# Down and output projections turned: weights held in the array, 512 tokens moving

## The chip, the cores and the metric

The kernel runs on one core of one Trainium2 chip. The metric is the device time of one launch in microseconds, as the median of several runs. Besides the runs there is a profile of one execution, with its trace, in which every instruction of every engine has a start and a length. The engines are TensorE (PE in the profile, with its weight loads as PEld), VectorE (DVE), ScalarE (ACT), GpSimd (POOL) and SyncE (SP). SP, ACT and POOL also issue DMA transfers, each in the order of its own queue. On chip, data lies in SBUF with 128 partitions; products of TensorE go to PSUM, whose eight banks of 128 x 512 fp32 the kernel hands round.

## The reference, cut to what matters

The input x has 2048 tokens of 640 features. A gate g per token mixes two branches: a is attention with a running memory over four segments of 512 tokens (32 heads of 20 features), b is a SwiGLU network with 1728 hidden features.

```python
def _A_ref(x, wq, wk, wv, wo, beta):        # H = 32, Dh = 20, N = 4, L = 512
    g = _sigmoid(beta).reshape(1, H, 1, 1)
    ...
    for s in range(N):
        logits = jnp.einsum("bhqd,bhkd->bhqk", qs, ks) * scale + mask
        p = _softmax(logits, axis=-1)
        a_dot = jnp.einsum("bhqk,bhkd->bhqd", p, vs)
        num = jnp.einsum("bhld,bhde->bhle", pq, M)
        den = jnp.einsum("bhld,bhd->bhl", pq, z)[..., None] + 1e-6
        a_mem = num / den
        o = g * a_mem + (1.0 - g) * a_dot
        M = M + jnp.einsum("bhld,bhle->bhde", pk, vs)
        ...
    return o @ wo

def _B_ref(x, w1, w3, w2):
    h = _silu(x @ w1) * (x @ w3)
    return h @ w2

g = _sigmoid((x * gate_w).sum(-1, keepdims=True))
return g * a + (1 - g) * b
```

## The kernel before

Everything is fp32. A number is split into a high part that TensorE takes in its fp32r format and the remaining low part, and a product is three passes, high x high, high x low and low x high (`PASSES`). The parts of weights are made by ACT (a cast, L115) and POOL (a subtraction, L116). Weights come as rows of 640 columns: `w_add` plans one, a DMA on SP brings it into `wr`, `w_step` advances the loads and splits by a count of work done, and six split rows `W` exist at a time. POOL brings ten of the query and key rows itself (L172).

**What TensorE does.** Its order is written out: generators yield after a piece of work, and a loop weaves them. `head` holds the first projections of tokens 0 to 1023 (chunks 0 and 1, called A). Then four segments `segs` follow; each is a list of jobs (projections, SwiGLU up and down, output projections) between whose pieces slots of `attention()` are put, by a credit of estimated time. `tail` is what is left after the last attention. `braid` puts one step of a generator after every few of another, `chain` joins them. Chunks 2 and 3 (B) come in the second half.

**The other engines.** Their instructions are in the order that a scheduler with a timeline model gives them; those in `here(...)` keep the order of the program. Each engine and each queue is strictly in its order: an instruction that waits holds all behind it.

**SwiGLU down, `ffn_down` (L509 to L535).** Called for five groups of hidden blocks, `GROUPS`, four of three blocks of 128 and one of the last full block and the 64-row rest, and for two chunks each. A tile `f` is 128 tokens x 320 features, a bank in PSUM: the hidden values `ht` of 128 tokens are the weights of the array, and 320 columns of `W` move (L523). Each product with three passes counts three matmuls, the rest two. Four blocks of tokens and two halves make eight tiles per chunk. The first group's eviction is a copy scaled by `cgate` = 1 - g on ACT (L529), the others multiply by `cgate` and add on DVE (L531), into `acc` (128 tokens x 4 blocks x 640). The rooms for accumulators (`slot`, two) are shared with the values `V` of a chunk: V of chunk 2 takes the room of chunk 0's accumulator, chunk 3's accumulator that of chunk 1's, each once its stores have landed. At the very last group (chunks 2 and 3) each block of tokens is stored from SP (L535).

**Attention (`attention`, L717).** Scores `s` and `t`, exps on ACT (`P`, L611), masks by POOL selects (L615), the products `o` with the values (L625). The results, not yet divided by their row sums, go through `oq` to the DRAM buffer `od`, 32 rows a head of which row 20 holds the sums. The memory's transposes `mr` go to `qk` by small DMAs on ACT (L593). POOL loads `qk` (L549).

**Output projection (`oproj`, L744 to L783; `normalize`, L681).** `o_sums` reads the row sums `rs` of a chunk, `o_scale` takes their reciprocals times (1 - sigmoid(beta)) and splits them into three bf16 parts `rp`, and three DMAs on SP put these into `rR` (L668). `normalize` multiplies a constant 0/1 matrix `sel` with `rR` on TensorE (L687, a tile `rr` per block of 128 features): this spreads a head's factor over its 20 features. DVE multiplies `oall` by it (L688), and adds the memory's part (L693), which POOL has read back as `gm` (`load_memory`, L678) and TensorE has turned (`gt`, L692). For chunk 0 there is no memory. `part` splits 128 tokens at a time into `oT`; a tile `op` is 128 tokens x 320 features of 15 matmuls (L768), and DVE multiplies it by the gate and adds it to `acc` (L777).

**Gate.** The projection of values has one more column, gate_w. `v_blocks` takes exp(-x) of it, and makes `gate` = g and `cgate` = 1 - g, one number per token and so per partition.

**Store.** `store(c)` (L785) sends chunks 0 and 1 from POOL's queue, four DMAs of 128 tokens x 640 (L788). `store(0)` is braided into the last down of A and is followed by the projections of q and v of chunk 2; `store(1)` is braided into the first down of B.

## Time and profile before

| what | value |
|---|---|
| median of 3 runs | 1114.06 us (1112.69 to 1115.69) |
| the profiled execution | 1116.25 us |
| its span, first to last instruction | 1114.5 us |
| mean granted clock of TensorE | 0.998 of full speed |
| PE busy | 1098.6 us, 99% of the span |
| PEld, DVE, ACT, POOL busy | 909.3, 591.4, 463.4, 482.3 us |
| DMA | 151.96 MB in 84911 packets, mean 136 GB/s |

A group of instructions in the profile is a line, an engine, an operation, the tile written and the tiles read, with partitions x elements; then the count, the busy time in us and the mean of one in ns; behind the second bar the idle time of the engine just before them and what ended it. Matmuls overlap in these records, so their spacing is read from the chain or a timeline: start, length, what, and how many. A wait names the instruction that waited, what released it, the total in us, the times and the longest. A row of the view of windows has, for each engine, busy us and count (PE, PEld, DVE, ACT, POOL), then the granted clock, the share of DMA and GB/s.

### The profile page before, as it was taken

To read this page: it belongs to the slowest core of one execution; us is meant where nothing else is said; L and a number is where in the kernel's file an instruction comes from. 1 tells how busy PE (TensorE), PEld (TensorE's weight loads), DVE (VectorE), ACT (ScalarE), POOL (GpSimd) and SP (SyncE) were. 2 spreads that over 40 slices of the span, in tenths; PEclk is the share of its full clock that TensorE was granted. 3 is DMA by queue.
4 is the path that set the end of the run, shared out by engine and by line. 5 is a ranking of instruction groups with operands and counts; after the bars stand their busy time and mean duration, and the time that the engine had idled before them with its cause. 6 is when DMAs were issued, how large, how long until landed. Compare 5 with 4: busy or idle time off the path is not lost. (4 is left out here: it accounts for less than half of the span.)

```text
span 1114.5 us, 19295 instructions
## 1 busy us (share of the span) xinstructions
PE 1098.6 (99%) x6953; PEld 909.3 (82%) x6953; DVE 591.4 (53%) x1750; ACT 463.4 (42%) x956; POOL 482.3 (43%) x603
## 2 busy tenths in 40 slices
PE   9999999999999999999999999998999999999998
PEld 6988878877878888988977786788778778877988
DVE  5032564355655544565253677774557666651644
ACT  6255334553343233255255644435534344344040
POOL 5053445355364254354253436434653545444140
PEclk9999999999999999999999999999999999999999
DMA  9275943334265134435285867435753433432122
GB/s 330 83 237 206 267 115 93 83 96 128 59 149 118 51 84 125 121 94 189 94 265 207 297 187 177 115 115 161 170 128 104 115 93 100 115 104 76 49 60 95
DMA packets 84911, 151.96 MB, mean 136 GB/s; under 512 B 11344, under 2 KB 24144, under 8 KB 84816
## 3 DMA queue, kind: packets, MB, share of 16 engines
q1 hardware_dynamic: 60528, 103.40, 29.6%
q0 software_dynamic: 20832, 41.30, 16.1%
q10 hardware_dynamic: 3456, 6.03, 1.5%
q8 instruction: 55, 0.90, 0.3%
q14 instruction: 40, 0.33, 0.1%
HBM read 95.25 MB, written 54.53 MB: 134 GB/s over the span
## 5 line engine op out<-in xcount | busy, mean ns | idle before, releaser
L116 POOL TENSOR_TENSOR W<-wr,W 128x640 fp32r<-128x640 f32 (+1 forms) x126 | 197.4, 1571 | 289.3 <-ACT W L115 229.2
L579 DVE CUSTOM_DVE_ANT_0 junk<-s,mask 128x256 bf16<-128x256 f32 (+3 forms) x512 | 250.5, 489 | 113.0 <-PE s L572 81.4
L611 ACT ACTIVATE P<-t 128x512 f32<-128x512 f32 (+1 forms) x384 | 172.0, 539 | 128.4 <-PE t L605 125.7
L261 PE MATMUL g<-X,W 128*128 128x512 f32 x840 | 207.9, 397 | 0.7 <-ACT P L611 0.7
L523 PE MATMUL f<-W,ht 128*128 128x320 f32 x1312 | 201.9, 313 | 0.3 <-POOL W L116 0.3
L523 PEld LDWEIGHTS f<-W,ht 128*128 128x128 f32 x1312 | 195.9, 190 | 3.1 <-POOL W L116 0.6
L261 PE MATMUL u<-X,W 128*128 128x512 f32 x780 | 197.3, 399 | 0.0
L261 PEld LDWEIGHTS g<-X,W 128*128 128x128 f32 x840 | 155.8, 188 | 36.6 <-ACT P L611 0.9
L615 POOL TENSOR_SCALAR_AFFINE_SELECT P<-P 128x256 f32<-128x256 f32 x192 | 92.5, 492 | 199.0 <-ACT P L611 198.8
L261 PEld LDWEIGHTS u<-X,W 128*128 128x128 f32 x780 | 143.7, 188 | 34.6 <-ACT P L611 0.3
L115 ACT CAST W<-wr 128x640 fp32r<-128x640 f32 (+1 forms) x133 | 95.0, 727 | 111.7 <-PE u L261 27.5
L116 POOL TENSOR_TENSOR ht<-ft,ht 128x512 fp32r<-128x512 f32 x52 | 67.0, 1288 | 86.8 <-ACT ht L115 82.9
L531 DVE SCALAR_TENSOR_TENSOR acc<-f,cgate,acc 128x320 f32<-128x320 f32 x128 | 69.4, 548 | 42.1 <-PE f L523 41.6
L549 POOL DMA_DIRECT2D qk<-qkd x128 | 82.7, 648 | 1.9 <-PE t L605 1.7
L572 PE MATMUL s<-qk 60*128 60x256 f32 (+3 forms) x512 | 76.6, 345 | 1.0 <-DVE fu L492 1.0
L261 PE MATMUL k<-X,W 128*128 128x512 f32 x300 | 76.6, 402 | 0.7 <-ACT P L611 0.7
L625 PE MATMUL o<-P,vg 128*32 128x512 f32 (+3 forms) x1024 | 75.5, 436 | 0.1
L261 PE MATMUL q<-X,W 128*128 128x512 f32 x300 | 73.8, 399 | 0.6 <-DVE X L116 0.4
L768 PE MATMUL op<-W,oT 128*128 128x320 f32 x480 | 74.0, 312 | 0.0
L372 PE MATMUL v<-W,X 128*128 128x320 f32 (+1 forms) x480 | 71.6, 311 | 1.1 <-ACT P L611 1.1
L372 PEld LDWEIGHTS v<-W,X 128*128 128x128 f32 x480 | 71.0, 189 | 1.5 <-ACT P L611 1.3
L768 PEld LDWEIGHTS op<-W,oT 128*128 128x128 f32 x480 | 71.1, 189 | 0.8
(105 smaller groups left out, 1025.3 us busy)
## 6 DMA issues: line engine op xcount, KB each, us to landing
qk<-qkd POOLq DMA_DIRECT2D x128, 240.0 KB, 4.5
wr<-in_w_dram SPq DMA_DIRECT2D x80, 320.0 KB
qkd<-qs SPq DMA_DIRECT2D x20, 512.0 KB
qkd<-ks SPq DMA_DIRECT2D x20, 512.0 KB
od<-oq SPq DMA_DIRECT2D x32, 256.0 KB
wr<-in_wo_dram SPq DMA_DIRECT2D x20, 320.0 KB
vg<-vd SPq DMA_DIRECT2D x16, 336.0 KB
xr<-in_xT_dram SPq DMA_DIRECT2D x20, 256.0 KB
```

Source lines behind the costliest of these rows:

```text
L115: pin(nc.scalar.copy(dst[:, 0], src))
L116: (lo or nc.gpsimd.tensor_sub)(dst[:, 1], src, dst[:, 0].bitcast(F32))
L261: nc.tensor.matmul(ps, w[:, a, kb * P:(kb + 1) * P], x[:, b, kb, :], start=n == 0, stop=n == 14)
L372: nc.tensor.matmul(ps[:, :n1 - n0], x[:, a, kb, lb * P:(lb + 1) * P], wvt[kb][:, b, n0:n1], start=n == 0, stop=n == 14)
L523: nc.tensor.matmul(ps[:, :320], a, b, start=n == 0, stop=n == len(ms) - 1)
L549: here(nc.gpsimd.dma_start(t[64 * i:64 * i + RH], qkd[c][RH * (h + i):RH * (h + i + 1)]))
L572: nc.tensor.matmul(ps[i][:, o:o + w], q[:, qb * P:(qb + 1) * P], key[:, :w], start=n == 0, stop=n == len(todo) - 1, skip_group_check=True)
L579: nc.vector.tensor_tensor_reduce(out=junk[:, :w], in0=ps[i][:, o:o + w], in1=mask[:, L - w:], scale=1.0, scalar=-3.0e38, op0=ALU.add, op1= ...
L611: last["exp"] = nc.scalar.activation(pairs[2 * m + k]["P"][:, i, o:o + n], ps[i][:, b:b + n], AF.Exp, scale=SCALE)
L615: nc.gpsimd.affine_select(d, d, pattern=[[0, 2], [0, n], [1, P]], base=0, channel_multiplier=-1, compare_op=ALU.is_ge, fill=0.0)
L625: nc.tensor.matmul(ps[32 * i:32 * i + 32, kb * P:], heads[2 * p + i]["v"][:, kb], pairs[p + i // 2]["P"][:, i % 2, o:o + n], start=kb == 0 ...
L768: nc.tensor.matmul(ps[:, :320], oT[0][:, qb % 2, a, kb * P:(kb + 1) * P], ws[kb][:, b, 320 * hf:320 * hf + 320], start=n == 0, stop=n == 14)
```

## The change

The two products that end in `acc` change sides. In the down projection 128 output features of `W` are now the weights of the array and the 512 tokens of a chunk move, so a tile is 128 features x 512 tokens, five a chunk (`fb`) for eight; the output projection does the same with `op`. `acc` is 128 x 5 x 512, and the output leaves the chip as chunk, block, feature, token; it is turned back on the host.

A token is now an element of a row and no partition, so the gate can no longer be a factor per partition. Instead of g and 1 - g the kernel keeps e = exp(x) (at most 1e10) and the share s = 1/(1 + e) = 1 - g. Then g a + (1 - g) b = s (e a + b). The ratio e is folded into what becomes a: into the memory's part when it is read (`memory_read`, a second factor of the same instruction) and into the factors of the row sums (`o_scale`). At the end `acc` is multiplied by s. Both go through a small DRAM buffer `ed` (a transfer of 4-byte pieces on ACT's queue) and are read back spread over the partitions: `er`, e for 32 heads, and `sh`, s for 128 partitions (`load_share`).

The factors of the row sums are no longer spread by a product: `o_scale` writes each head's factors 20 times to the DRAM buffer `rd` by four DMAs, and `normalize` reads blocks of 128 rows of it (`rb`), in the same two buffers that `sh` uses. `gm` is loaded by block of features; `oT`'s high parts take its room, the low parts that of `oall`.

For chunks 0 and 1 `store` loads the share, and POOL multiplies each of the five blocks and issues its DMA. For chunks 2 and 3 the last group of `ffn_down` adds, multiplies (alternately on POOL and DVE) and stores from SP; the last tile is done in two halves on DVE.

```diff
...
                 nc.vector.reciprocal(r, r)
-                nc.vector.tensor_mul(
-                    gm.rearrange("p (h e) -> p h e", e=DH),
-                    nd[:, :, :DH], r.unsqueeze(2).broadcast_to([P, 16, DH]))
+                nc.vector.scalar_tensor_tensor(
+                    gm.rearrange("p (h e) -> p h e", e=DH), nd[:, :, :DH], gate[:, c, 1, qb:qb + 1],
+                    r.unsqueeze(2).broadcast_to([P, 16, DH]), op0=ALU.mult, op1=ALU.mult)
                 store_later(gd[c][:, qb, 320 * hf:320 * hf + 320], gm, ("g", c, qb), n=2)
...
                 if hf == 1:
-                    nc.scalar.activation(gate[:, c, lb:lb + 1], ps[:, 320:321], AF.Exp, scale=-1.0)
+                    nc.scalar.activation(gate[:, c, 1, lb:lb + 1], ps[:, 320:321], AF.Exp)
                 yield 450
             store_later(vd[c][:, lb], vv.rearrange("p h e -> p (h e)"), ("v", c, lb), nc.scalar)
-        nc.vector.tensor_scalar(gate[:, c], gate[:, c], 1.0, None, op0=ALU.add)
-        nc.vector.reciprocal(gate[:, c], gate[:, c])
-        nc.vector.tensor_scalar(cgate[:, c], gate[:, c], -1.0, 1.0, op0=ALU.mult, op1=ALU.add)
+        e, g = gate[:, c, 1], gate[:, c, 0]
+        nc.vector.tensor_scalar(e, e, TOP, None, op0=ALU.min)
+        nc.vector.tensor_scalar(g, e, 1.0, None, op0=ALU.add)
+        nc.vector.reciprocal(g, g)
+        store_later(ed[c].rearrange("x a p -> p (x a)"), gate[:, c].rearrange("p x a -> p (x a)"), ("e", c), nc.scalar)
     def k_block(c, mb, i, prev):
...
             if first:
-                accs[c] = slot(f"acc{c}")[:, :4 * D].rearrange("p (b d) -> p b d", b=4)
-            for lb in range(4):
-                for hf in range(2):
-                    ps = bank_tile(f"f{c}_{js[0]}_{lb}_{hf}", 700)
-                    ms = []
-                    for j, w in zip(js, w2s):
-                        for a, b in (PASSES if j < NF else ((0, 0), (0, 1))):
-                            ms.append((hts[c, j][:, a, lb * P:(lb + 1) * P], w[:, b, 320 * hf:320 * hf + 320]))
-                    for n, (a, b) in enumerate(ms):
-                        nc.tensor.matmul(ps[:, :320], a, b, start=n == 0, stop=n == len(ms) - 1)
-                        if n == len(ms) // 2:
-                            yield 149.0 * (n + 1)
-                    filled()
-                    dst = accs[c][:, lb, 320 * hf:320 * hf + 320]
-                    if first:
-                        nc.scalar.activation(dst, ps[:, :320], AF.Copy, scale=cgate[:, c, lb:lb + 1])
-                    else:
-                        nc.vector.scalar_tensor_tensor(dst, ps[:, :320], cgate[:, c, lb:lb + 1], dst,
-                                                       op0=ALU.mult, op1=ALU.add)
-                    yield 149 * (len(ms) - len(ms) // 2 - 1)
-                if last:
-                    nc.sync.dma_start(out[0, c * L + lb * P:c * L + lb * P + P, :], accs[c][:, lb])
+                accs[c] = slot(f"acc{c}")[:, :KB * L].rearrange("p (b n) -> p b n", b=KB)
+            if last:
+                load_share(c)
+            for fb in range(KB):
+                ps = bank_tile(f"f{c}_{js[0]}_{fb}", 1300 if len(js) > 2 else 690)
+                ms = []
+                for j, w in zip(js, w2s):
+                    for a, b in (PASSES if j < NF else ((0, 0), (0, 1))):
+                        ms.append((w[:, b, fb * P:(fb + 1) * P], hts[c, j][:, a, :]))
+                for n, (w, h) in enumerate(ms):
+                    nc.tensor.matmul(ps, w, h, start=n == 0, stop=n == len(ms) - 1)
+                    if n % 3 == 2 and n < len(ms) - 1:
+                        yield 699.0 if n == 2 else 699
+                filled()
+                dst = accs[c][:, fb]
+                if first:
+                    nc.scalar.copy(dst, ps)
+                elif not last:
+                    nc.vector.tensor_add(dst, ps, dst)
+                else:
+                    end = (c, fb) == (cs[-1], KB - 1)
+                    for n0 in ((0, 256) if end else (0,)):
+                        d, p, g = (t[:, n0:n0 + (256 if end else L)] for t in (dst, ps, shares[c]))
+                        nc.vector.tensor_add(d, p, d)
+                        (nc.vector if end or fb % 2 else nc.gpsimd).tensor_mul(d, d, g)
+                        nc.sync.dma_start(out[c, fb, :, n0:n0 + d.shape[-1]], d)
+                yield 699 if len(ms) % 3 == 0 else 466
     oall, heads, pairs = {}, {}, {}
...
     def o_sums(c):
+        assert ("e", c) in stored
         here(nc.sync.dma_start(rs, od[c][:, DH].rearrange("h (a n) -> h a n", n=P)))
+        here(nc.sync.dma_start(er, ed[c][1:2].broadcast_to([H, 4, P])))
         after(16 if c < NSEG - 1 else 3, o_scale, c)
...
         if b == 0:
-            oall[c] = cp.tile([P, KB, L], F32, tag="oall", name=f"oall{c}", bufs=1)
+            oall[c] = cp.tile([P, KB, L], FR, tag="oall", name=f"oall{c}", bufs=1)
         for h, e, n, r in rows(b):
-            dst = oall[c][r:r + n, b]
+            dst = oall[c][r:r + n, b].bitcast(F32)
             if n > DH:
...
         here(nc.vector.reciprocal(rs, rs))
-        nc.vector.tensor_scalar(rs, rs, cR, None, op0=ALU.mult)
-        nc.vector.tensor_copy(rp[:, 0], rs)
-        nc.vector.tensor_sub(rs, rs, rp[:, 0])
-        nc.vector.tensor_copy(rp[:, 1], rs)
-        nc.vector.tensor_sub(rp[:, 2], rs, rp[:, 1])
-        for i in range(3):
-            here(nc.sync.dma_start(rR[32 * i:32 * i + 32].rearrange("h (a n) -> h a n", n=P), rp[:, i]))
+        nc.vector.scalar_tensor_tensor(rs, rs, cR, er, op0=ALU.mult, op1=ALU.mult)
+        for a in range(4):
+            here(nc.sync.dma_start(rd[c][:, :, a * P:(a + 1) * P], rs[a::4].unsqueeze(1).broadcast_to([H, DH, P])))
         turned.append(c)
+    shares = {}
+    def spread(name):
+        return sp.tile([P, L], F32, tag="spread", name=name, bufs=2)
+    def load_share(c):
+        shares[c] = spread(f"sh{c}")
+        here(nc.sync.dma_start(shares[c], ed[c][0].rearrange("a n -> (a n)").unsqueeze(0).broadcast_to([P, L])))
     gms = {}
...
         assert ("g", c, 3) in stored
-        gms[c] = big_tile(f"gm{c}")[:, :4 * D].rearrange("p (b d) -> p b d", b=4)
+        gms[c] = big_tile(f"gm{c}", FR)[:, :KB * L].rearrange("p (b n) -> p b n", b=KB)
         for qb in range(4):
-            here(nc.gpsimd.dma_start(gms[c][:, qb], gd[c][:, qb]))
+            here(nc.gpsimd.dma_start(gms[c].bitcast(F32)[:, :, qb * P:(qb + 1) * P],
+                                     gd[c][:, qb].rearrange("p (b n) -> p b n", b=KB)))
             yield 1
     def normalize(c):
+        rows = rd[c].rearrange("h e n -> (h e) n")
+        rb = {}
+        def load(b):
+            if b < KB:
+                assert c in turned
+                rb[b] = spread(f"rb{c}_{b}")
+                here(nc.sync.dma_start(rb[b], rows[b * P:(b + 1) * P]))
+        load(0)
+        load(1)
+        yield 1
+        if not c:
+            gms[c] = big_tile(f"oT{c}", FR)[:, :KB * L].rearrange("p (b n) -> p b n", b=KB)
         for b in range(KB):
-            assert c in turned
-            o = oall[c][:, b]
-            ps = bank_tile(f"rr{c}_{b}")
-            nc.tensor.matmul(ps, sel[:, b * P:(b + 1) * P], rR, start=True, stop=True)
-            nc.vector.tensor_mul(o, o, ps)
+            o, hi = rb[b], gms[c][:, b]
+            nc.vector.tensor_mul(o, oall[c][:, b].bitcast(F32), o)
             if c:
...
                 for qb in range(4):
-                    nc.tensor.transpose(pt[:, qb * P:(qb + 1) * P], gms[c][:, qb, b * P:(b + 1) * P], ident)
+                    nc.tensor.transpose(pt[:, qb * P:(qb + 1) * P], hi[:, qb * P:(qb + 1) * P].bitcast(F32), ident)
                 nc.vector.tensor_add(o, o, pt)
-            yield 700
+            nc.scalar.copy(hi, o)
+            nc.vector.tensor_sub(oall[c][:, b], o, hi.bitcast(F32))
+            load(b + 2)
+            yield 450 if c else 1
     NJ = NSEG * H
...
         ws, oT = [], []
-        def part(qb):
-            if qb == 0:
-                oT.append(big_tile(f"oT{c}", FR)[:, :4 * D].rearrange("p (q a n) -> p q a n", q=2, a=2))
-            split(oT[0][:, qb % 2].rearrange("p a (b n) -> p a b n", n=P), oall[c][:, :, qb * P:(qb + 1) * P],
-                  lo=nc.vector.tensor_sub)
         def first():
             yield from normalize(c)
-            yield 1
-            part(0)
-            part(1)
+            oT.extend((gms[c], oall[c]))
         def rest():
             ws.extend(w_get(i, plan[0]) for i in plan)
-            for qb in range(4):
-                for hf in range(2):
-                    ps = bank_tile(f"op{c}_{qb}_{hf}", 800)
-                    n = 0
-                    for kb in range(KB):
-                        for a, b in PASSES:
-                            nc.tensor.matmul(ps[:, :320], oT[0][:, qb % 2, a, kb * P:(kb + 1) * P],
-                                             ws[kb][:, b, 320 * hf:320 * hf + 320], start=n == 0, stop=n == 14)
-                            n += 1
-                        if (qb, hf) == (3, 1):
-                            clock["oldest"] = plan[kb] + 1
-                        if kb in (1, 3):
-                            yield 890
-                    filled()
-                    dst = accs[c][:, qb, 320 * hf:320 * hf + 320]
-                    nc.vector.scalar_tensor_tensor(dst, ps[:, :320], gate[:, c, qb:qb + 1], dst,
-                                                   op0=ALU.mult, op1=ALU.add)
-                    yield 450
-                if qb < 2:
-                    part(qb + 2)
+            for fb in range(KB):
+                ps = bank_tile(f"op{c}_{fb}", 1300)
+                n = 0
+                for kb in range(KB):
+                    for a, b in PASSES:
+                        nc.tensor.matmul(ps, ws[kb][:, b, fb * P:(fb + 1) * P], oT[a][:, kb], start=n == 0, stop=n == 14)
+                        n += 1
+                    if fb == KB - 1:
+                        clock["oldest"] = plan[kb] + 1
+                    if kb < KB - 1:
+                        yield 699
+                filled()
+                dst = accs[c][:, fb]
+                nc.vector.tensor_add(dst, ps, dst)
+                yield 699
         return first(), rest()
-    def store(c, qb=None):
-        o = out[0, c * L:(c + 1) * L, :].rearrange("(b p) d -> p b d", p=P)
-        for qb in range(4):
-            here(nc.gpsimd.dma_start(o[:, qb], accs[c][:, qb]))
+    def store(c):
+        load_share(c)
+        yield 1
+        for fb in range(KB):
+            d = accs[c][:, fb]
+            nc.gpsimd.tensor_mul(d, d, shares[c])
+            here(nc.gpsimd.dma_start(out[c, fb], d))
             yield 1
...
     r = _run(nc, [arrays], core_ids=[0])
-    return r.results[0]["out_0_dram"]
+    return _np.ascontiguousarray(_np.asarray(r.results[0]["out_0_dram"]).transpose(0, 3, 1, 2)).reshape(1, S, D)
```

More of the change, by code (lines that the diff above doesn't have):

```diff
@@ L49, in gated_mix @@
     gd = [dp.tile([P, 4, D], F32, name=f"gd{c}") for c in range(NSEG)]
+    ed = [dp.tile([2, 4, P], F32, name=f"ed{c}") for c in range(NSEG)]
+    rd = [dp.tile([H, DH, L], F32, name=f"rd{c}") for c in range(NSEG)]
     ident = cp.tile([P, P], F32, name="ident")
@@ L57, in gated_mix @@
     cR = cp.tile([P, 1], F32, name="cR")
[L58 removed]
     rs = cp.tile([P, P], F32, name="rs")
[L60 to L61 removed]
+    er = cp.tile([P, P], F32, name="er")
     nsT = [cp.tile([P, 32], FR, name=f"ns{i}") for i in range(2)]
[L63 to L64 removed]
+    gate = cp.tile([P, NSEG, 2, 4], F32, name="gate")
     Ms = {}
@@ L802, in job_down @@
     def job_down(cs, g, last=False):
-        return 2.384 * sum(3 if j < NF else 2 for j in GROUPS[g]), ffn_down(cs, GROUPS[g], plan_down(GROUPS[g]), last)
+        return 2.32 * sum(3 if j < NF else 2 for j in GROUPS[g]), ffn_down(cs, GROUPS[g], plan_down(GROUPS[g]), last)
     def jobs_up(cs, g):
```

20 lines of the change are left out of this document (3 added, 17 removed).

## The prediction

> **What bounds the kernel now.** I read the page first, then the table of TensorE's waits, the chain that ended last, and last the timelines of POOL and ACT around the places where output is stored.
>
> ```profile
> span 1114.5 us, 19295 instructions
> PE 1098.6 (99%) x6953; PEld 909.3 (82%) x6953; DVE 591.4 (53%) x1750; ACT 463.4 (42%) x956; POOL 482.3 (43%) x603
> ...
> L523 PE MATMUL f<-W,ht 128*128 128x320 f32 x1312 | 201.9, 313 | 0.3 <-POOL W L116 0.3
> L768 PE MATMUL op<-W,oT 128*128 128x320 f32 x480 | 74.0, 312 | 0.0
> ```
>
> PE is busy for 99% of the span, every other engine for about half. So a microsecond leaves the span only if a matmul leaves PE, and enters it only if PE waits or runs slower. What PE waits for now, as engine and line, then total, times, longest:
>
> ```profile
> PE nd L339 <- ACT P L611: 3.6, 1, 3.6
> PE t L605 <- DMA qk<-mr: 1.8, 1, 1.8
> PE v L372 <- ACT P L611: 1.1, 1, 1.1
> PE f L523 <- POOL W L116: 0.3, 1, 0.3
> ```
>
> The chain (start, length, what) gives the true spacing of matmuls; the mean durations above (313 ns) overlap and are no spacing:
>
> ```profile
> 1048.60 0.23 PE rr L687
> ...
> 1052.58 0.23 PE rr L687
> ...
> 1059.87 10.44 PE g L261 x45
> ...
> 1099.24 11.60 PE f L523 x77
> 1110.85 0.02 issue
> 1110.87 0.55 DVE acc L531
> ```
>
> A 512-wide fp32r matmul takes 10.44/45 = 0.232 us. The 320-wide f takes 11.60/77 = 0.151 us here, and 0.147 in a stretch ahead of the output projection:
>
> ```profile
> 1035.33 13.27 PE f L523 x90
> ```
>
> I take 0.148, between the two, for f and op alike. Per column that is 0.46 ns against 0.45.
>
> **The change, part by part.**
>
> *Turned products.* Down: 41 products x 2 halves x 4 blocks x 4 chunks = 1312 matmuls of 320 become 41 x 5 blocks x 4 = 820 of 512: 820 x 0.232 = 190.2 for 1312 x 0.148 = 194.2, so -4.0 (-1.4 at 0.146, -7.4 at 0.1506). Output: 480 x 0.148 = 71.0 becomes 300 x 0.232 = 69.6, so -1.4 (-0.5 to -2.7).
>
> The Trainium skill ("TensorE: Matmul & The Clock Gate", Back-to-back issue gap) gives an isolated gap of N/2.4 + 2.5 ns: 215.8 ns for 512 columns, 135.8 for 320. By that, an estimate, both parts together would save 1.2 + 0.4 = 1.6 us. The trace has 232 and 148, both higher, and decides.
>
> *Row sums.* The 20 rr matmuls go: 20 x 0.23 = -4.6, all on PE. The four gt transposes per block stay, so they cost nothing new. PE total: -4.0 - 1.4 - 4.6 = -10.0.
>
> *Waits that go.* The 0.3 on the last W: the last output tile becomes 15 x 0.232 = 3.5 us long and lets the weight buffer go earlier before its end. -0.3.
>
> *VectorE and ScalarE.* Evictions become fewer and wider; the chain of casts in front of rr goes. Both engines have half their time free, and no wait of PE above names their evictions: 0 on the path, and 0 if they were slower by a third. First evictions move one line but stay on ACT.
>
> *The end.* Today the last eviction takes 0.55 and its store closes the span at 1114.5, 3.65 after PE's end at 1110.85. Changed, a last tile is 5 matmuls = 1.16 us, and DVE has to add, multiply by the share and only then issue. By the rows below, a 512-wide two-input operation is 0.68 and a 256-wide one some 0.4 (estimate by width). In DVE's order the multiplications of tiles 1 and 3 come after tile 3's addition, so 0.2 + 0.7 remain of these when PE ends, then 4 x 0.42: the last issue at PE's end + 2.6 against + 0.55. The last transfer is 128 KB instead of 320 KB, -0.3. Net +1.8 (+0.5 if the multiplications come earlier, +3.5 if the share of the last chunk, loaded behind chunk 2's stores on SP, lands late).
>
> ```profile
> L688 DVE TENSOR_TENSOR oall<-oall,rr 128x512 f32<-128x512 f32 x20 | 13.7, 682 | 4.7 <-PE rr L687 4.7
> L116 POOL TENSOR_TENSOR ht<-ft,ht 128x512 fp32r<-128x512 f32 x52 | 67.0, 1288 | 86.8 <-ACT ht L115 82.9 <-DMA rR<-rp 3.9
> L788 POOL DMA_DIRECT2D out_dram<-acc x8 | 4.5, 563 | 0.5 <-DVE acc L531 0.5
> ```
>
> These are groups of instructions by form (busy us, mean ns). The view of the output stores' line adds the time from issue to landing:
>
> ```profile
> DMA to landing us min/median/max: 3.3/4.7/5.8
> ```
>
> *Store of chunk 1.* This is where I expect most to be lost. Today POOL issues four stores back to back (first fence), which land about 4.7 after the last issue at 761.7, near 766.4. ACT's first eviction of chunk 3 into the accumulator that chunk 1 leaves comes at 770.78, 4 us later, and waits for PE alone (POOL's and ACT's timelines: start, length, line, what, and in brackets the idle time before it):
>
> ```profile
> 759.98 2.23 POOL L788 DMA_DIRECT2D out_dram<-acc  x4
> 762.95 1.02 POOL L615 TENSOR_SCALAR_AFFINE_SELECT P<-P 128x256 f32<-128x256 f32 x2 [0.74 <-ACT P L611]
> 764.08 1.35 POOL L549 DMA_DIRECT2D qk<-qkd  x2
> ```
> ```profile
> 770.78 0.53 ACT L529 ACTIVATE acc<-f,cgate 128x320 f32<-128x320 f32 x1 [0.79 <-PE f L523]
> 772.09 0.53 ACT L529 ACTIVATE acc<-f,cgate 128x320 f32<-128x320 f32 x1 [0.78 <-PE f L523]
> 772.82 1.58 ACT L611 ACTIVATE P<-t 128x512 f32<-128x512 f32 x3 [0.20 <-PE t L605]
> ```
>
> Changed, each store follows a POOL multiplication: 5 x 1.29 = 6.45 us, not startable before the share has been loaded (one more load on SP behind a weight and a vg load; I put its landing at 762.6, one out-store's 4.7 after it can be issued). In POOL's order two selects (1.02) and two qk issues (1.35) sit among them, then five issues of 0.56: the last near 762.6 + 6.45 + 1.02 + 1.35 + 4 x 0.56 = 773.6, landed at 777.0 to 778.3 (3.3 to 4.7). The first eviction of chunk 3 waits for all five stores, and the exps of the woven attention are queued behind it on ACT. PE goes on until it needs that bank or one of these exps, by its order near 773.5. Stall 3.5 to 4.8: I take +4.5. Bounds: 0 (the share earlier, other work between) and +7.
>
> A stall that long costs twice. After the 3.6 us of idle time ahead of the matmul at 755.18 the next f matmuls ran slowly:
>
> ```profile
> 755.18 0.99 PE nd L339 x6
> 756.17 4.92 PE f L523 x23
> ```
> ```profile
> 746.00:757.00 11.00, 7.41 (x71) 5.34 (x70) 5.97 (x19) 5.89 (x13) 7.22 (x8) 0.97 0.44 130
> 757.00:775.00 18.00, 18.00 (x138) 16.09 (x137) 6.63 (x30) 8.92 (x19) 8.03 (x14) 0.92 0.68 194
> ```
>
> 23 x 0.148 would be 3.4 us, it took 4.92, and the granted clock (the third number from the right) of the second window is 0.92: 18 x 0.08 = 1.4 us lost. So +1.0 for a stall near this length (0 or 1.5). The Trainium skill ("TensorE: Matmul & The Clock Gate", What's actually happening) says that PE falls to half clock after an idle window of some 3.4 us; the trace agrees (3.6 idle, clock 0.92 behind it).
>
> *Store of chunk 0.* Today its four issues stand between the down tiles at 501 to 505, the V memset that waits for them runs at 507.82, and V's first copy comes much later:
>
> ```profile
> 504.50 0.54 POOL L788 DMA_DIRECT2D out_dram<-acc  x1 [0.47 <-DVE acc L531]
> 507.82 0.37 POOL L358 MEMSET V<- 128x128 f32 x1 [2.78 <-DMA out_dram<-acc]
> 509.14 3.10 POOL L116 TENSOR_TENSOR W<-wr,W 128x642 fp32r<-128x642 f32 x2 [0.95 <-ACT W L115]
> ...
> 517.37 1.56 POOL L116 TENSOR_TENSOR W<-wr,W 128x640 fp32r<-128x640 f32 x1 [1.14 <-ACT W L115]
> ```
> ```profile
> 517.83 6.47 PE L372 MATMUL v<-W,X 128*128 128x320 f32 x42 [1.08 <-ACT P L611]
> ```
>
> Changed, five multiplications (6.45) and five issues (2.8) come after the down and ahead of the low halves of V's weights on POOL, so the weights come some 2 to 3 us late for v, and the memset waits for the last store until about 521. v's wait of 1.1 becomes some 4.3: +3.2 (0 to +5).
>
> *Gate.* The ratio, its 4-byte pieces, er and the shares' loads add DMA issues on ACT and SP (0.33 to 0.6 each) that lie beside PE: 0. *Spread.* Per chunk, 2560 pieces of 512 B out and 1.3 MB back in, with the two spread buffers holding SP's later weight loads until DVE has multiplied. Mostly under projections: +0.7, my allowance (0 to +5, a rival below).
>
> *Sum:* -10.0 - 0.3 + 1.8 + 4.5 + 1.0 + 3.2 + 0.7 = +0.9 on the profiled execution, which took 1116.25 around its span of 1114.5. The three runs have 1112.69 to 1115.69, median 1114.06, so this execution stands 2.2 above the median. On the median: 1114.06 + 0.9 = 1115.
>
> **Rivals.**
>
> *Faster: the stores stay hidden.* If POOL's multiplications come before their place, or PE has other banks and exps for some 5 us, the 8.7 us of the two stores shrink to about 1: 1115 - 8 = 1107. For it: today's margins are 12 us (memset 507.82, first copy after 517.83) and 4 us (766.4, 770.78). Against: POOL gets 6.45 us of work exactly in front of the stores, and its order is one queue.
>
> *Slower: the spread's pieces hold the memory's transposes.* PE waits 1.8 us already for qk<-mr in front of attention at 685, and the factors of chunk 1 leave SP at the same time:
>
> ```profile
> L593 ACTq DMA_DIRECT2D qk<-mr x2: 517/521/525, 679.2 to 679.8; - x2
> ...
> 685.23 0.73 PE L605 MATMUL t<-qk 62*128 62x512 f32 x6 [1.76 <-DMA qk<-mr]
> ```
> ```profile
> q1 hardware_dynamic: 60528, 103.40, 29.6%
> ```
>
> A packet of SP's queue takes 0.296 x 1114.5 x 16 / 60528 = 87 ns on the mean; 2560 of them over 16 engines are 13.9 us if a short piece costs as much as a mean one, 4 at its share of bytes. It decides once mr lands after 685.2, where nothing else is woven. With 4 to 5 us there, half clock behind it included: 1115 + 4.5 = 1119.5. Against: mr is on another queue, and is tiny.
>
> *No gain on the array.* If the turned products pace no better per column than the 320-wide ones do (0.148 x 512/320 = 0.237), the 5.4 us of the turned products go and only the 4.6 of the row sums stay: 1115 + 5.4 = 1120. Against: the chain's rows, where the projections do run at 0.232 with a new weight tile for each matmul. By the issue gap of the Trainium skill's page named above, 1.6 of the 5.4 would be left: 1119.
>
> **Chances.** A measurement here tells about 0.3%, 3.3 us, from no change. Forecast 0.36 (own range 1111 to 1118), stores hidden 0.30, spread in the way 0.26, no gain on the array 0.08. Faster: 0.30 and a little of the forecast, 0.33. Same: most of the forecast, 0.31. Slower: the other two and a little, 0.36. The range takes in 1107 and 1120, with a microsecond on each side for the end's bounds: 1106 to 1121.
>
> **What would show it.** f spacing 0.232 and no rr: right on the array. The table of waits must name v (or q) behind ACT near 515 to 522 and the chunk 3 eviction held by out stores near 773 to 778, with a clock below 1 behind it. The end: the last DVE operation some 2.6 after the last matmul. Wrong if those stalls are absent, if t waits longer for qk<-mr, or if DVE hangs on rb loads and PE waits for it.

## The result and the profile after

The changed kernel takes 1164.23 us (median of 4 runs, 1161.55 to 1166.73) where the kernel before takes 1114.88 (4 runs). The ratio is 1.0438, 95% interval 1.0399 to 1.0477: 4.4% slower, far outside the range of 1106 to 1121 that was forecast.

From the page of the changed kernel (span; busy us, share and instructions of each engine; TensorE's clock in 40 slices; one group):

```profile
span 1159.6 us, 17915 instructions
PE 1104.2 (95%) x6261; PEld 860.8 (74%) x6261; DVE 582.0 (50%) x1685; ACT 460.4 (40%) x948; POOL 505.1 (44%) x615
PEclk8989999999999999999999998998999999999999
L515 PE MATMUL f<-ht,W 128*128 128x512 f32 x820 | 197.3, 398 | 0.0
```

PE has 692 matmuls fewer (f alone 820 for 1312) and is busy 5.6 us longer. Its clock line has an 8 in four slices, two of them in the first 90 us, where the kernel before had none; the mean clock is 0.979 for 0.998. The first of these slices is no part of the waits below: it lies at 0 to 29 us, ahead of all of them. What PE waited for:

```profile
PE o L620 <- ACT acc L521: 9.0, 1, 9.0
PE k L250 <- ACT P L606: 6.9, 1, 6.9
PE pm L417 <- ACT pkn L404: 6.2, 1, 6.2
PE g L250 <- DVE m L574: 3.3, 1, 3.3
PE o L620 <- POOL P L610: 3.2, 1, 3.2
PE t L600 <- DMA qk<-mr: 3.1, 1, 3.1
PE v L361 <- POOL W L105: 2.6, 2, 1.4
```

The worst wait was 3.6 us; now six are near that or far above it. In the order of these rows they end at 808, 581, 77, 719, 922 and 706 us, so they are no single event. The chain at the end (start, length, what):

```profile
1148.24 3.65 DMA sh<-ed
1151.89 0.03 issue
1151.92 0.02 DVEq L529
1151.94 0.04 issue
1151.98 2.36 DVE acc L529 x2
1154.35 0.67 DVE acc L528 x2
1155.01 0.74 DVE acc L529
```

The last matmul ends near 1151.1 (its line's last start, 1150.7, and 0.4 for it), 8.5 us ahead of the span's end; before it was 3.7. So the 45.1 us of span are made of three: PE stands idle 46.9 us ahead of its last matmul (1151.1 - 1104.2) for 12.2 (1110.8 - 1098.6), +34.7; its work takes 5.6 more, although the matmuls should have saved 10; and the end is 4.8 longer. None of the three is the size of the turned matmuls' gain: PE's work of 1104.2 us holds stretches at a lower clock. The question for the experiments is which part of the change makes PE wait.

### The profile page after: what moved, and what is told of

The parts are those of the page before. It is cut to its first block, busy times and chain, and to the rows that moved or that the text cites. A ratio compares the mean times of both kernels' runs of the same rounds, so it can differ in the third digit from the quotient of the medians.

```text
span 1159.6 us, 17915 instructions
## 1 busy us (share of the span) xinstructions
PE 1104.2 (95%) x6261; PEld 860.8 (74%) x6261; DVE 582.0 (50%) x1685; ACT 460.4 (40%) x948; POOL 505.1 (44%) x615
## 5 line engine op out<-in xcount | busy, mean ns | idle before, releaser
L250 PE MATMUL g<-X,W 128*128 128x512 f32 x840 | 211.2, 401 | 4.3 <-DVE m L574 3.3
L515 PE MATMUL f<-ht,W 128*128 128x512 f32 x820 | 197.3, 398 | 0.0
L515 PEld LDWEIGHTS f<-ht,W 128*128 128x128 f32 x820 | 153.4, 189 | 36.5
L620 PE MATMUL o<-P,vg 128*32 128x512 f32 (+3 forms) x1024 | 79.4, 452 | 12.3 <-ACT acc L521 9.0
L544 POOL DMA_DIRECT2D qk<-qkd x128 | 83.1, 651 | 12.8 <-PE t L600 12.7
L250 PE MATMUL q<-X,W 128*128 128x512 f32 x300 | 76.7, 410 | 1.5 <-ACT W L104 1.0
L620 PEld LDWEIGHTS o<-P,vg 128*32 128x32 f32 x1024 | 31.2, 113 | 56.5 <-issue 34.6
L523 DVE TENSOR_TENSOR acc<-f,acc 128x512 f32<-128x512 f32 x70 | 48.0, 689 | 47.5 <-PE f L515 47.4
L250 PEld LDWEIGHTS q<-X,W 128*128 128x128 f32 x300 | 57.3, 194 | 17.6 <-ACT W L104 1.5
```

The costliest lines, as they stand in the source:

```text
L250: nc.tensor.matmul(ps, w[:, a, kb * P:(kb + 1) * P], x[:, b, kb, :], start=n == 0, stop=n == 14)
L515: nc.tensor.matmul(ps, w, h, start=n == 0, stop=n == len(ms) - 1)
L523: nc.vector.tensor_add(dst, ps, dst)
L544: here(nc.gpsimd.dma_start(t[64 * i:64 * i + RH], qkd[c][RH * (h + i):RH * (h + i + 1)]))
L620: nc.tensor.matmul(ps[32 * i:32 * i + 32, kb * P:], heads[2 * p + i]["v"][:, kb], pairs[p + i // 2]["P"][:, i % 2, o:o + n], start=kb == 0 ...
```

## The experiments

Three suspects came from the places of the waits: the 4-byte store of e and the share (two waits stand right behind it), the spread of the factors by DMA (the waits from 700 to 720 and near 920), and the shares' loads ahead of store and end. The rival to all three was that the new order of work, not a transfer, makes PE wait.

### The 4-byte store alone, put into the kernel before

```diff
+        nc.vector.tensor_copy(both[:, c, 0], gate[:, c])
+        nc.vector.tensor_copy(both[:, c, 1], cgate[:, c])
+        store_later(ed[c].rearrange("x a p -> p (x a)"), both[:, c].rearrange("p x a -> p (x a)"), ("e", c), nc.scalar)
```

> The kernel before with one part of the change alone: it also writes its two gate factors per chunk to a DRAM buffer that nobody reads, 1024 pieces of 4 bytes on ACT's queue at the place where the changed kernel writes e and the share (two small copies on VectorE in front). Theory 1 (the 4-byte pieces clog the DMA engines, so that weight loads behind them land late): slower by 10 to 22 us, with PE waiting for ACT near 65 to 75 us and again near 570 us, and the granted clock below 1 in the first 100 us. Rival (those two waits come from the turned order of work, not from the pieces): within 3 us of before, no such waits.

Measured: 1133.56 us, ratio 1.0173 (1.0153 to 1.0193). 19 us for four stores that nobody reads. The waits are the changed kernel's, at the same places (75 and 581 us):

```profile
PE k L263 <- ACT P L616: 9.2, 1, 9.2
PE pm L431 <- ACT pkn L418: 6.9, 1, 6.9
```

Windows of 60 to 64 and 64 to 72 us (the last three numbers are PE's clock, the share of the DMA engines and GB/s), first the kernel before, then with the store at 60:

```profile
60.00:64.00 4.00, 4.00 (x21) 3.30 (x20) 1.36 (x2) 3.49 (x6) 1.00 (x1) 1.00 0.97 351
64.00:72.00 8.00, 8.00 (x42) 6.49 (x42) 2.08 (x3) 4.58 (x10) 4.66 (x6) 1.00 0.62 210
```
```profile
60.00:64.00 4.00, 4.00 (x19) 3.25 (x18) 1.36 (x2) 1.72 (x3) 0.76 (x2) 1.00 1.01 179
64.00:72.00 8.00, 3.65 (x18) 2.65 (x17) 0.00 (x0) 0.73 (x1) 1.56 (x1) 0.99 0.95 48
```

For 8 us the DMA engines are busy 95% of the time and move 48 GB/s for 210. (The view's DMA share can come out above 1, as in one row here.) The queue of SP in the same 64 to 72 us (packets, MB, share of 16 engines), first before, then with the store:

```profile
q1 hardware_dynamic: 824, 1.67, 61.7%
```
```profile
q1 hardware_dynamic: 191, 0.39, 94.5%
```

So a packet of SP's loads and stores, 2 KB, takes 633 ns on the mean (94.5% x 16 x 8 us / 191) for 96. The 4-byte pieces are not among them: their queue, ACT's, has no packet left in this window. What is slow is everybody else's traffic after them. On SP's queue three stores take 12.28 us to issue for 3.84, and ACT's cast stands 6.30 us behind a late weight:

```profile
60.73 3.84 SPq L280 DMA_DIRECT2D qkd<-ks  x3
```
```profile
61.62 12.28 SPq L282 DMA_DIRECT2D qkd<-ks  x3
```
```profile
72.29 0.72 ACT L117 CAST W<-wr 128x640 fp32r<-128x640 f32 x1 [6.30 <-DMA wr<-in_wqk_dram]
```

### The store turned, in the changed kernel

```diff
+        for g4 in range(4):
+            nc.vector.transpose(gT[:, 32 * g4:32 * g4 + 32], gates_[32 * g4:32 * g4 + 32, 8 * c:8 * c + 32])
-        store_later(ed[c].rearrange("x a p -> p (x a)"), gate[:, c].rearrange("p x a -> p (x a)"), ("e", c), nc.scalar)
+        store_later(ed[c].rearrange("x a p -> (x a) p"), gT[:8], ("e", c), nc.scalar)
```

> The changed kernel with e and the share turned on VectorE first (four 32x32 transposes of 0.2 us a chunk), so that the store is 8 pieces of 512 B for 1024 of 4 B. Theory 1: the waits of 6.2 us (pm behind ACT) and 6.9 us (k behind ACT) go and the clock of the first 100 us returns to 1.00: 15 to 22 us faster than the changed kernel, 1142 to 1149. Rival: less than 3 us faster.

Measured: 1143.91 us, ratio 1.0271 (1.0242 to 1.03): 20.3 less than the changed kernel. pm's wait is gone, k's is 0.7, and the clock of the first 100 us is 1.00 for 0.93. Of these 0.07 only half belongs to the store: in the changed kernel the windows 0 to 30 and 60 to 90 us have 0.89 each, and the first lies ahead of the first store at 43.7. In the run above, with the store alone, the first 100 us have 0.97. The store is shown as a cause from both sides. Gains over the changed kernel are differences of two medians of four runs, each with an interval of 0.3 to 0.4% to either side, so they are good to some 5 us.

### How many pieces, and where they go

Two more runs of the kernel before with the store: only one of the factors (512 pieces), and all 1024 pieces with 512 B between them.

```diff
-        ... ed[c].rearrange("x a p -> p (x a)"), both[:, c].rearrange("p x a -> p (x a)")
+        ... ed[c][0].rearrange("a p -> p a"), both[:, c, 0]
```

> As the run of the kernel before with the store of 4-byte pieces (19 us slower), but with only one of the two factors written: 512 pieces a chunk for 1024. If each small write costs the memory its own time: the loss is halved, 8 to 11 us slower than before. If it is a threshold (a full queue): either nothing, within 3 us, or nearly the whole 19.

```diff
-    ed = [dp.tile([2, 4, P], F32, name=f"ed{c}") for c in range(NSEG)]
+    ed = [dp.tile([2, 4, P, P], F32, name=f"ed{c}") for c in range(NSEG)]
-        ... ed[c].rearrange("x a p -> p (x a)"), ...
+        ... ed[c][:, :, :, 0].rearrange("x a p -> p (x a)"), ...
```

> As the run with 1024 pieces of 4 B, but each piece goes to a row of its own, 512 B from the next, where they lie side by side in the first run. If it is the neighbouring pieces that collide in the memory (many writers to the same few bytes): little is lost, within 5 us of before. If each small write costs by itself, wherever it goes: the same 17 to 21 us.

Measured: half of them 1131.24 us, ratio 1.0151 (1.0133 to 1.0169), nearly the whole loss, so the loss is not in proportion to the pieces; all of them apart 1114.94, ratio 1.001 (1.0 to 1.0019), no loss. The windows of the last, and the row of ACT's queue from 60 to 64 us, which is the same with the pieces side by side and apart:

```profile
60.00:64.00 4.00, 4.00 (x19) 3.19 (x18) 1.36 (x2) 2.48 (x5) 0.96 (x2) 1.00 0.84 251
64.00:72.00 8.00, 8.00 (x44) 6.66 (x42) 1.61 (x3) 4.94 (x10) 4.48 (x5) 1.00 0.71 238
```
```profile
q10 hardware_dynamic: 1040, 0.00, 14.6%
```

It is not the number or the size of the pieces alone, since 1024 pieces of 4 B cost nothing here. It is where they land: side by side in 4 KB, or spread over 512 KB. Whether the pieces must touch or only fall into the same few KB, these runs do not tell. Nor is it time that the pieces themselves take: in both runs they take 9 ns each on the mean (14.6% x 16 x 4 us / 1040). Why the packets of the other queues are slow for some 8 us behind them no trace here shows. The Trainium skill ("DMA: Bandwidth & Descriptors", Specifications) says that transfers below 512 B are done as read-modify-write. By itself this does not tell the two runs apart, since both write 4 B.

### The spread by DMA alone, put into the kernel before

```diff
-            nc.tensor.matmul(ps, sel[:, b * P:(b + 1) * P], rR, start=True, stop=True)
-            nc.vector.tensor_mul(o, o, ps)
+            nc.vector.tensor_mul(o, o, rb[b])
...
+            load(b + 2)
```

with `rd`, `spread` and the four DMAs of `o_scale` as in the changed kernel.

> The kernel before with one part of the change alone: the row sums' factors go by DMA (2560 pieces of 512 B out, five blocks of 256 KB back in two buffers) and the 20 products rr are gone. Theory 2 (the spread holds SP's queue and the memory's transposes and makes DVE wait): what it saves on PE, 4.6 us, is lost again and more, 2 to 10 us slower than before, 1116 to 1125, with t waiting longer for qk<-mr near 680 to 700 us and PE waiting for a DVE that waits for rb. Rival (the spread is as cheap as it looks, only the rest of the change hurts): 3 to 5 us faster, 1110.

Measured: 1122.37 us, ratio 1.0074 (1.0057 to 1.0091): 8.1 slower, though 20 matmuls of 0.23 are gone. So the spread costs about 12.7. Of this, t's wait for qk<-mr is no part (1.3 us here, 1.8 before): the time was forecast right, and so was the VectorE that waits for rb, but t was the wrong victim. Its waits:

```profile
PE g L248 <- DVE m L566: 5.6, 1, 5.6
PE nd L326 <- ACT P L598: 1.7, 1, 1.7
PE s L559 <- DVE ft L485: 1.4, 1, 1.4
...
DVE oall L680 <- DMA rb<-rd: 15.6, 11, 3.2
```

and VectorE's timeline ahead of g's wait (in brackets the idle time before):

```profile
693.60 0.69 DVE L680 TENSOR_TENSOR oall<-oall,rb 128x512 f32<-128x512 f32 x1 [0.49 <-DMA rb<-rd]
695.93 0.88 DVE L680 TENSOR_TENSOR oall<-oall,rb 128x512 f32<-128x512 f32 x1 [1.42 <-DMA rb<-rd]
...
697.54 2.07 DVE L680 TENSOR_TENSOR oall<-oall,rb 128x512 f32<-128x512 f32 x1
```
```profile
697.51 1.54 POOL L103 TENSOR_TENSOR W<-wr,W 128x640 fp32r<-128x640 f32 x1
```

VectorE is in the middle of the maxima of the scores when the multiplication's factors have not come; the maxima behind it wait, and PE's banks with them. Two buffers mean that the third load cannot start before the first multiplication is done. That is not all of g's 5.6 us (695.9 to 701.6): two of the multiplications take 0.88 and 2.07 us for 0.69, 1.6 more in all, while POOL works beside them, the second beside a POOL subtraction that started 0.03 us earlier. The kernel before had no such multiplication here, since its factors `rr` come from PSUM, while `oall` and `rb` both lie in SBUF. Behind the wait the clock is 0.71 from 700 to 710 us.

### The factors written once, repeated by the reads

```diff
-        for a in range(4):
-            here(nc.sync.dma_start(rd[c][:, :, a * P:(a + 1) * P], rs[a::4].unsqueeze(1).broadcast_to([H, DH, P])))
+        here(nc.sync.dma_start(rd[c].rearrange("h (a n) -> h a n", n=P), rs))
...
-                here(nc.sync.dma_start(rb[b], rows[b * P:(b + 1) * P]))
+                for h, e, n, r in rows(b):
+                    m = max(n // DH, 1)
+                    src = rd[c][h:h + m].unsqueeze(1).broadcast_to([m, n // m, L])
+                    here(nc.sync.dma_start(rb[b][r:r + n], src))
```

> The changed kernel with the factors of the row sums written once (128 pieces of 512 B a chunk for 2560) and repeated 20 times by the reads instead (11 loads a chunk for 5). Theory 2 (the 2560 short pieces hold SP and the memory's transposes near 700 us): t's wait of 3.1 and g's of 3.3 near 705 to 720 shrink, 4 to 10 us faster, about 1157. Rival (the reads back, not the writes, hold DVE and SP; 11 issues are worse than 5): within 3 us or slower.

Measured: 1174.56 us, ratio 1.0543 (1.0508 to 1.0577), 10 us slower than the changed kernel. A miss for theory 2 as I had put it, and the rival's case: more reads back hurt. They are 52 issues of 0.70 us for 20 of 0.32, and VectorE waits 31.9 us for them where it waited 19.7 (first the changed kernel, then this run). Since the run made the writes fewer and the reads more, it does not show whether the 2560 pieces written cost anything.

```profile
L693 SPq DMA_DIRECT2D rb<-rd x20: 319/320/1337, 394.5 to 1103.8; - x20
```
```profile
DVE rb L702 <- DMA rb<-rd: 19.7, 12, 3.6
```
```profile
L694 SPq DMA_DIRECT2D rb<-rd x52: 514/704/800, 394.0 to 1115.0; - x52
```
```profile
DVE rb L703 <- DMA rb<-rd: 31.9, 15, 5.4
```

### The shares loaded early

```diff
+            for s in {0: (0,), 1: (1,), 3: (2, 3)}.get(c, ()):
+                load_share(s)
             ws.extend(w_get(i, plan[0]) for i in plan)
```

and no `load_share` in `store` and `ffn_down`.

> The changed kernel with each share loaded at the start of an output projection (chunks 0 and 1 in their own, 2 and 3 in the last) instead of right ahead of its use. Theory 3 (the share's load queued on SP late is what makes the end and the store of chunk 1 long): the end after PE's last matmul falls from 8 us of waiting for the last share to some 5 in all, and the wait of 9.0 us behind ACT's eviction near 800 us falls to 3 to 5: 12 to 17 us faster, 1147 to 1152. Rival (POOL's 6.3 us of multiplications in front of the stores are the price): the end gains, the 9.0 us stays, 8 to 10 us faster.

Measured: 1146.39 us, ratio 1.0275 (1.0247 to 1.0304), 17.8 less than the changed kernel. The wait of 9.0 is gone and not only shortened, both waits of v are gone, and the end is 5.3 us (last matmul near 1139.9, span 1145.2) for 8.5. In the changed kernel the share of chunk 1 was issued at 784.94, and POOL's five multiplications started 6.8 us later (SP's and POOL's timelines of the changed kernel):

```profile
784.94 0.61 SPq L671 DMA_DIRECT2D sh<-ed  x1
```
```profile
791.72 6.28 POOL L794 TENSOR_TENSOR acc<-acc,sh 128x512 f32<-128x512 f32 x5 [6.57 <-DVE m L574]
...
800.23 2.77 POOL L795 DMA_DIRECT2D out_dram<-acc  x5
```

The bracket names VectorE, whose update came last; it was the share that POOL waited for, since the last of the sixteen marks of its landing stands at 791.57 in the trace. With the share early POOL multiplies as long as before and nothing waits for it, so its 6.3 us, which the rival blamed, are hidden if they start in time.

### Both edits, and the products back

> The changed kernel with the two edits together: e and the share turned before they are stored, and the shares loaded early. Alone they gained 20.3 and 17.8 us. If they are separate queues' waits they add: 1126. Rival (one of the two hides behind the other): 1132 or more.

1127.09 us, ratio 1.0119 (1.01 to 1.0139). The two gains add: 1164.2 - 20.3 - 17.8 = 1126.1. Then, on top of both, the products `rr` in place of the spread (with them, chunk 0's share is loaded ahead of the last down of A, and the places of `normalize` in the weave move a little):

```diff
-        for a in range(4):
-            here(nc.sync.dma_start(rd[c][:, :, a * P:(a + 1) * P], rs[a::4].unsqueeze(1).broadcast_to([H, DH, P])))
+        nc.vector.tensor_copy(rp[:, 0], rs)
+        ...
+            here(nc.sync.dma_start(rR[32 * i:32 * i + 32].rearrange("h (a n) -> h a n", n=P), rp[:, i]))
...
-            nc.vector.tensor_mul(o, oall[c][:, b].bitcast(F32), o)
+            nc.tensor.matmul(ps, sel[:, b * P:(b + 1) * P], rR, start=True, stop=True)
+            nc.vector.tensor_mul(o, oall[c][:, b].bitcast(F32), ps)
```

> As the run with the two edits, and the factors of the row sums again spread by the 20 products of the kernel before, not by DMA (the turned products, the ratio and the shares stay; shares and the divided blocks use the room of f tiles). Theory 2: PE gets 4.6 us back to do, but the waits near 690 to 720 and 905 to 925 and the half clock behind them go: 6 to 12 us faster than the run with two edits, 1114 to 1120 if that one has 1126. Rival (the waits there come from other parts): 4 to 5 us slower than it.

1118.0 us, ratio 1.0038 (1.0023 to 1.0053): 9 less, with 4.6 us more for PE to do, so the spread cost some 13.7 here and 12.7 in the kernel before. The three parts account for the loss but for 0.4% of the time.

### What is left: the end, and a wait that swallows

```diff
-                        nc.vector.tensor_add(d, p, d)
-                        (nc.vector if end or fb % 2 else nc.gpsimd).tensor_mul(d, d, g)
+                        here(nc.vector.tensor_add(d, p, d))
+                        here((nc.vector if end or fb % 2 else nc.gpsimd).tensor_mul(d, d, g))
...
-        after(16 if c < NSEG - 1 else 3, o_scale, c)
+        after(22 if c < NSEG - 1 else 3, o_scale, c)
```

> The run with two edits and the products, with two further edits: in the last group each multiplication follows its addition in program order, and the factors of the row sums are made 22 slots after their load for 16, so that the small transposes for chunk 2's memory stand ahead of them on VectorE. Theory 4 (what the turned products save ahead of 685 us is swallowed there, because t waits for qk<-mr, whose transposes stand behind VectorE's wait for rs): t's wait of 3.4 us shrinks below 1 and the end shortens by about 1: 1113 to 1115. Rival (the 22 slots only move the wait to rr, whose factors come later): 1117.

> The kernel before with the one number changed, 22 slots for 16 ahead of the factors of the row sums. Theory 4: its 1.8 us wait of t for qk<-mr goes, 1 to 2 us faster, within 0.2%. Rival: no change, or slower by the wait of rr.

The first took 1116.33 us, ratio 1.0013 (1.0 to 1.0026); the second 1113.63, ratio 0.9995 (0.9982 to 1.0007), no change to be told. t's wait for qk<-mr went only from 3.4 to 2.5 and from 1.8 to 1.1 us, not below 1 in the first: theory 4 holds at most in part, and these runs do not settle how much the early savings lose there. In the first the last matmul ends near 1108.8 in the profiled execution, 2 us ahead of that of the kernel before; its end of 5.7 us eats that. So the share was moved off the end:

```diff
+                if c > 1 and j in GROUPS[4]:
+                    nc.vector.tensor_mul(u, u, shares[c])
...
-                        here((nc.vector if end or fb % 2 else nc.gpsimd).tensor_mul(d, d, g))
```

and the accumulators of chunks 2 and 3 are multiplied ahead of the last group, with both shares loaded at the start of `tail`.

> The run with the products, the ordered end and the 22 slots, and the share is moved off the end for chunks 2 and 3: the hidden values of the last group are multiplied by it before their split, and the accumulators ahead of the last group (VectorE and POOL, beside matmuls), so that the last group only adds and stores. If the two operations after the last addition are what the end has more than before: the time from PE's last matmul to the span's end falls from 5.8 us to 3.5 or so, 1113 to 1114.5, level with the kernel before or up to 0.2% ahead. Rival (the rest of the end is the stores' own, five of them close together): no change, 1116.

1114.06 us, ratio 1.0001 (0.9988 to 1.0014), and the end is 3.7 us as before. Span, engines and the chain's end:

```profile
span 1111.4 us, 17969 instructions
PE 1094.8 (99%) x6281; PEld 854.1 (77%) x6281; DVE 590.8 (53%) x1721; ACT 460.1 (41%) x948; POOL 508.3 (46%) x620
...
1096.19 11.55 PE f L537 x50
1107.73 0.02 issue
1107.76 0.42 DVE acc L552
```

PE is busy 3.8 us less than before at the same mean clock (0.998), with the 20 products still there, and this span is 3.1 shorter than the 1114.5 of the kernel before, while the medians of the two kernels are level. The two profiled executions do not stand alike: this one is 0.9 below its median, the one before 2.2 above. A part of the gain seems to go in the clock: of the 12 executions four have a mean clock of 0.995 and one has 1.000, where of the 17 of the kernel before in the same comparison none is under 0.997 and six have 1.000. At the same 0.998 the median is 1113.1 (5 executions) for 1114.7 (8). Why the clock is lower more often was not tested; t waits longer here (3.0 for 1.8). This is the best form of the change that was found, and it does not beat the kernel before.

## Why the prediction was wrong

- **Turned products, -5.4.** Mechanism and size were right. The last 50 f of the best version take 11.55 us, 0.231 each. Added up from start to start of the matmuls in the traces, f and op take 266.1 us in the best version and 264.5 to 264.6 in the two versions before it, for 270.8 to 271.2 in the kernel before, the one with 22 slots and the one with the pieces apart: 4.7 to 6.7 less. By the issue gap of the Trainium skill ("TensorE: Matmul & The Clock Gate", Back-to-back issue gap) it would have been 1.6, an estimate; the rows were the better guide. (At 0.146 the sum for the down products gives -1.3, not -1.4.)
- **The gate, "that lie beside PE: 0".** This step failed, a term put at nothing. I counted the issues of the 4-byte store (0.38 us on ACT) and not what the transfers do to the others behind them: packets of SP's queue at 633 ns for 96, a weight that ACT waits 6.3 us for, PE idle for 6.9 and 9.2 us. It cost 19.0 us alone in the kernel before and 20.3 in the changed one: more than the whole range allowed. No row of the trace before had a store of that kind, so 0 was not a bound from rows; the small store nearest to it, mr's, is 8 KB and no pattern like it.
- **The spread, +0.7 "my allowance".** It failed in size: 12.7 us in the kernel before, 4.6 of which the lost products gave back; the range for it ended at +5. The rival named for it, t behind qk<-mr, was not it (1.3 us). The sign named last in the prediction was: VectorE hangs on rb, and PE waits for VectorE. What the prediction did not have is that the multiplication by rb, both operands in SBUF, is also slower beside POOL.
- **Store of chunk 1, +4.5.** The mechanism was right to the queue: the eviction on ACT waits for the out stores, and PE's o behind it. The size was 9.0, beyond the bound of +7. From the share's landing to the end of ACT's wait it was 15.4 us (791.57 to 806.98), where the prediction had 14.4 to 15.7 (762.6 to 777.0 and 778.3): that part of the sum was right. The mis-sized term is the head start ahead of PE's need: 10.9 us in the prediction (762.6 to 773.5), 7.0 in the run (791.57 to 798.6, where PE's wait begins). Of the 3.9 us between, 1.9 is the share's landing, 6.6 us after its issue for 4.7; the rest, a later issue or an earlier need of PE, was not taken apart. With the share early the whole wait vanished, which is the bound 0 that the prediction named for that case.
- **Store of chunk 0, v's wait 4.3.** The size was right, 2.6 behind POOL's W and 1.5 behind ACT, 4.1 in all, but in part by luck. The prediction blamed POOL's multiplications and issues alone. POOL also sat idle for 3.8 us for the share, with the low halves of V's weights behind it; with the share early it multiplies as long, and both waits of v are gone.
- **The clock, +1.0.** Right in kind, too small since it was charged once. With the long stalls come slow stretches: 60 to 90 us, with pm's 6.2, has a clock of 0.89, for 1.00 when that wait is gone. By the mean clock, 0.979 for 0.998 over 1160 us, about 22 us of full speed were withheld; part of that fell in the stalls themselves, and some in 0 to 30 us (0.89), where none of the named waits lies.
- **The end, +1.8.** It was +4.8, beyond the upper bound of +3.5. The case named for that bound, a late last share, is what happened (3.65 us in the chain); two multiplications that took 2.36 us beside POOL came on top. The order of VectorE was as told.

The three failures have one root. Every term that I worked out from instructions was near or right in kind; the terms that I called covered were transfers (the 4-byte store, the spread, the share's loads), and I had no price for them, or one from another kind of transfer.

## What to carry to other kernels

Before a value per partition is turned into a row by a DMA of single elements, turn it on an engine: four VectorE transposes of 0.2 us replaced a store that cost 19 us, although the store itself took 0.4 us to issue. A load that is new on a strictly ordered queue should be issued where its source is ready, not where its value is used; here that alone was worth 17.8 us. When a matmul is replaced by a transfer, price the engine that will wait for the transfer with other work queued behind it: 4.6 us of products were cheaper than 12.7 of waits and slowed work.

## What the runs showed that was not expected

- After 1024 writes of 4 B side by side the other queues are slow: 64 to 72 us had the DMA engines busy 95% at 48 GB/s. With 512 B between the pieces, the same 1024 of them cost nothing that can be measured (1.001, 1.0 to 1.0019). With half as many pieces, still side by side, the loss was 16.7 us for 19.0, two numbers whose intervals overlap.
- VectorE and POOL slow each other in the end of the changed kernel: VectorE's two 512-wide multiplications took 2.36 us, 1.18 each on the mean for 0.69 alone, while two on POOL took 3.44, 1.72 each for 1.29. VectorE's additions of a product from PSUM keep their 0.69 beside a POOL multiplication (at 1141.89 and 1144.19); what is slowed, here and in the spread's 2.07, are operations of VectorE with both operands in SBUF, though not each of them: in the run of the spread one beside two of POOL's selects took 0.70 (at 891.47).

```profile
1151.98 2.36 DVE L529 TENSOR_TENSOR acc<-acc,sh 128x512 f32<-128x512 f32 x2 [1.34 <-DMA sh<-ed]
1152.03 3.44 POOL L529 TENSOR_TENSOR acc<-acc,sh 128x512 f32<-128x512 f32 x2 [4.19 <-DMA sh<-ed]
```
